# A re-planned token-and-channel mixer: one load waits for another, a copy of r goes ahead of casts of v, weight loads go ahead of batch 1's loads

## The chip, the cores and the metric

The kernel runs on one NeuronCore of one Trainium2 chip. The metric is the device time of one execution in microseconds (us). The changed kernel is compared with the kernel before by the medians of repeated executions on the same chip.

## What is computed

Four batches of a linear attention with decay (RWKV style; 8 heads, 768 steps, 48 features per head) feed an MLP mixer of token and channel parts. Cut to what matters:

```python
for t in range(S):                                   # S = 768
    kt, vt, rt = k[:, :, t], v[:, :, t], r[:, :, t]
    cur = einsum('bhd,bhe->bhde', u * kt, vt)
    y[:, :, t] = einsum('bhd,bhde->bhe', rt, state + cur)
    state = w * state + einsum('bhd,bhe->bhde', kt, vt)
x = y as (4, 768, 8 * 48 = 384)
h = (relu(x.T @ w_tok1) @ w_tok2).T                  # 768 -> 256 -> 768 over the steps
u = x + h
out = u + relu(u @ w_ch1) @ w_ch2                    # 384 -> 1536 -> 384
```

All inputs and the output are float32 in HBM.

## The kernel before

**Units.** A batch is cut into 6 chunks of 128 steps; batches and chunks are counted from 0, as in the code (the title of the change calls them one, two). A chunk needs k, v and r: tiles `kt`, `vt` (192 KB each) and, in batches 0 and 1, `win`, which holds r of two chunks (384 KB); in batches 2 and 3 `rt` (192 KB). k and r are scaled by tables of powers of w (`kr`), turned (by TensorE through `trk` and `tr_ps` in batches 0 and 1, by a DMA transpose into `rk` later), and copied out of PSUM as `rka` (k) and `rkb` (r). v is cast to `vb`. Then come the scores `at_ps`, masked to `AT` on DVE, the state `kv_ps` kept as `S`, the chunk's own step (`adg`, then `ydb` or `yd`), and `y_ps`, which is copied to `x_b`.

**Mixer.** A batch's six `x_b` go through the hidden layer (`hid`: 12 matmuls of 384 columns on `h_ps<-x_b,wtok`), back (`hx_ps` or `hT_ps`, then `uT`), 24 *up* steps (three matmuls `z_ps<-uT,wch` each and a relu to `zr`), and 18 *down* steps (four matmuls `h_ps<-wch,zr` each), then the sum `osb` and a store. The mixer of one batch is what TensorE does between the short attention steps of the next.

**Weights.** Seven loads on GpSimd's queue, which also cast to bf16: W0 and W1 (`wtok`), W2 (`wch`, columns of w_ch1 for the first 4 of 12 up steps of a half), W3 (the other 8, 768 KB), W4, W5, W6 (`wch`, a third of w_ch2 each). All but W3 are 384 KB. The hidden layer needs W0, back needs W1, up steps need W2 or W3, a down step needs one of W4 to W6.

**What sets the order.** Everything is a task of a static plan: ORDER is the order in which the tasks are written out, and each engine then executes its own instructions in that order and waits at the first one that isn't ready. ENGINES says which engine takes a task that two could do, BUFS which buffer it writes, FILL puts a few matmuls on zeros ahead of some early tasks. Three more tables add waits between DMAs, from landing to issue: HOLD makes a load wait for another load, W_DEP makes a weight load wait for a load, GATES makes a load wait for a weight load. A load is written (batch, chunk, i), with i = 0 for k, 1 for r, 2 for v. All loads, the DMA transposes and nearly all stores share SP's queue; the weight loads stand on POOL's, between its products. A wait of one load therefore holds all that stand behind it on SP.

Of the kernel before, what the change touches and what calls it, by code (L numbers as in the profile page):

```python
# [63 lines left out]
    0, 1, 2, 0, 1, 0, 2, 1, 0, 2, 1, 0, 2, 1, 0, 1, 2, 1, 0, 2, 1, 0, 2, 1,  # L64
],
    'AT1': [
    0, 1, 2, 0, 1, 0, 2, 1, 0, 2, 0, 1, 2, 1, 0, 1, 2, 0, 1, 2, 0, 1, 2, 0,
# [11 lines left out]
    0, 1, 2, 3, 4, 1, 0, 2, 3, 4, 1, 0, 2, 3, 4, 0, 1, 2, 3, 0, 4, 1, 2, 3,  # L79
# [5 lines left out]
    0, 1, 2, 3, 4, 5, 0, 1, 4, 2, 3, 0, 4, 5, 1, 2, 0, 3, 5, 1, 4, 2, 0, 3, 5, 1, 2, 0, 4, 3,  # L85
],
    'kt': [
    0, 1, 2, 3, 4, 5, 0, 1, 2, 3, 4, 5, 0, 1, 2, 3, 4, 5, 0, 2, 1, 3, 4, 5,
],
    'ku': [  # L90
    0, 1, 2, 0, 1, 0, 2, 0, 1, 2, 0, 1,
# [12 lines left out]
],  # L104
    'osb': [
    0, 1, 2, 0, 1, 2, 2, 1, 0, 1, 2, 2, 0, 1, 2, 0, 1, 0, 2, 0, 1, 2, 0, 1, 2,
# [5 lines left out]
    0, 1, 2, 3, 0, 1, 2, 3, 1, 0, 2, 3,  # L112
],
    'rka': [
    0, 1, 2, 0, 1, 2, 0, 1, 2, 0, 1, 2,
# [5 lines left out]
    0, 1, 1, 0, 1, 1, 0, 1, 0, 1, 0, 1,  # L121
],
    'rt': [
    0, 1, 2, 3, 4, 0, 1, 2, 3, 0, 4, 2,
],
    'uT': [
    0, 1, 2, 3, 1, 0, 3, 2,
# [5 lines left out]
    0, 1, 2, 3, 4, 0, 1, 3, 2, 4, 0, 1, 3, 2, 4, 3, 1, 0, 2, 3, 4, 1, 0, 3,  # L133
],
    'vt': [
    0, 1, 2, 3, 4, 5, 0, 1, 3, 2, 4, 5, 0, 1, 3, 2, 5, 4, 0, 3, 1, 2, 4, 5,
# [5 lines left out]
    0, 1, 2, 0, 2, 1, 0, 2, 1, 2, 0, 2, 0, 1, 2, 0, 1, 2,  # L142
],
    'ydb': [
    0, 1, 0, 1, 0, 1,
# [5 lines left out]
ENGINES = [  # L151
# [9 lines left out]
]  # L161
W_DEP = [(0, 2, 2), (0, 5, 0), (0, 5, 0), (0, 3, 2), (1, 2, 0), (1, 1, 2), (1, 5, 0)]
HOLD = {(0, 4, 1): (0, 2, 1),
# [12 lines left out]
GATES = {(2, 0, 2): 1, (2, 4, 1): 3, (3, 1, 0): 2, (3, 1, 1): 6, (3, 5, 2): 5}  # L176
# [1058 lines left out]
```

## Time and profile before

| what | value |
|---|---|
| times of the kernel before | 163.26, 163.88, 171.22 us (median 163.88) |
| profiled execution, device time | 163.55 us |
| its span, first to last instruction | 161.8 us |
| around the span | 1.75 us |
| busy: PE, DVE, ACT, POOL | 153.7, 114.1, 68.3, 85.7 us |
| bytes moved by DMA | 26.89 MB |

The durations below come from the profiled execution, whose time is 0.33 us under the median. TensorE (PE) is the busiest engine. Its matmuls are pipelined, so the mean duration of one (326 ns for 384 columns) is longer than the step from one to the next (about 163 ns in a row of nine such matmuls that takes 1.46 us). All lines of the kernel read L282 in the profile, since a helper records every instruction; tiles tell them apart.

### The profile page before, as it was taken

The numbers are of one execution on the slowest core, as the hardware profiler recorded it, in microseconds if no ns is written. First come the engines' busy times: TensorE is split into PE (matmuls) and PEld (weight loads), VectorE is DVE, ScalarE is ACT, GpSimd is POOL, SyncE is SP. The second block draws the span as 40 slices with busy tenths as digits, with TensorE's granted clock in tenths as the row PEclk, the third lists the DMA queues.
The fourth block names the chain that finished last, engine by engine and source line by source line (L and its number), as shares of the span: only waits on it lengthen the run. The fifth ranks groups of instructions, "written<-read, shape, count | busy, mean of one in ns | idle before, by whom it ended". The sixth has DMA issues, their size and how long they took to land.

```text
span 161.8 us, 3784 instructions
## 1 busy us (share of the span) xinstructions
PE 153.7 (95%) x1459; PEld 102.2 (63%) x1459; DVE 114.1 (70%) x243; ACT 68.3 (42%) x153; POOL 85.7 (53%) x108
## 2 busy tenths in 40 slices
PE   6998789899999899999999999999999999999992
PEld 1465567567666677666677765677666666666671
DVE  6689874568888998598799927967899245743423
ACT  3989785727732441246146341046541202242200
POOL 7149892008581179999959895999924000000000
PEclk9999999999999999999999999999999999999999
DMA  4999899998989899999999799898990143500133
GB/s 126 202 205 182 138 236 222 209 231 165 231 153 221 177 203 175 239 199 145 199 237 203 173 234 169 169 233 177 170 267 21 48 88 131 150 26 0 44 142 106
DMA packets 93061, 26.89 MB, mean 166 GB/s; under 512 B 87794, under 2 KB 92148, under 8 KB 93044
## 3 DMA queue, kind: packets, MB, share of 16 engines
q1 hardware_dynamic: 90688, 23.40, 70.6%
q0 software_dynamic: 2160, 3.15, 11.3%
q8 instruction: 11, 0.18, 0.5%
q10 hardware_dynamic: 196, 0.11, 0.2%
q14 instruction: 6, 0.05, 0.1%
HBM read 20.46 MB, written 4.72 MB: 156 GB/s over the span
## 4 chain that ended last, share of the span: by engine, by line
PE 65%; DMA 22%; DVE 3%; ACT 3%; SPq 2%; issue 1%; POOL 1%; POOLq 0%
PE h_ps L282 30%; PE z_ps L282 24%; DMA wch<-in_moe_w_ch_dram 9%; DMA kt<-in_k_dram 8%; DMA vt<-in_v_dram 5%; PE hT_ps L282 3%; PE y_ps L282 3%; PE at_ps L282 3%; SPq L282 2%; DVE AT L282 2%; PE kv_ps L282 1%; PE hx_ps L282 1%; DVE S L282 1%; ACT vb L282 1%; POOL kr L282 1%
## 5 line engine op out<-in xcount | busy, mean ns | idle before, releaser
L282 PE MATMUL h_ps<-wch,zr 128*128 128x384 bf16 (+1 forms) x300 | 54.0, 319 | 0.7 <-DMA wch<-in_moe_w_ch_dram 0.5
L282 PE MATMUL z_ps<-uT,wch 128*128 128x384 bf16 x288 | 52.0, 326 | 0.6 <-DMA wch<-in_moe_w_ch_dram 0.6
L282 ACT ACTIVATE zr<-z_ps 128x384 bf16<-128x384 f32 x59 | 27.6, 494 | 46.8 <-PE z_ps L282 39.4
L282 PEld LDWEIGHTS <-wch 128*128 128x128 bf16 x288 | 31.4, 114 | 13.8 <-DMA wch<-in_moe_w_ch_dram 1.0
L282 PEld LDWEIGHTS <-zr 128*128 128x128 bf16 x300 | 27.3, 97 | 16.0 <-issue 0.7
L282 DVE TENSOR_TENSOR AT<-at_ps,mask 128x512 bf16<-128x512 f32 x48 | 31.1, 683 | 5.4 <-PE at_ps L282 5.2
L282 DVE TENSOR_SCALAR zr<-z_ps 128x384 bf16<-128x384 f32 x37 | 19.6, 552 | 10.6 <-PE z_ps L282 9.5
L282 POOL TENSOR_TENSOR kr<-kt,wnat 128x384 bf16<-128x384 f32 x19 | 18.9, 1003 | 3.2 <-DMA kt<-in_k_dram 2.5
L282 POOL TENSOR_TENSOR yd<-vb,adg 128x384 f32<-128x384 bf16 x15 | 12.4, 834 | 8.7 <-DVE adg L282 3.9
L282 DVE TENSOR_TENSOR osb<-u_sb,h_ps 128x384 f32<-128x384 bf16 (+1 forms) x16 | 8.2, 525 | 10.7 <-PE h_ps L282 10.4
L282 PEld LDWEIGHTS <-kr 128*128 128x128 bf16 x176 | 12.0, 103 | 5.6 <-POOL kr L282 2.2
L282 ACT CAST vb<-vt 128x384 bf16<-128x384 f32 x19 | 9.6, 512 | 8.7 <-DMA vt<-in_v_dram 8.7
L282 POOL TENSOR_TENSOR rku<-ku,rt 128x384 f32<-128x384 f32 x12 | 12.0, 1012 | 1.0 <-DVE adg L282 0.9
L282 POOL TENSOR_TENSOR kr<-rt,wp 128x384 bf16<-128x384 f32 x12 | 12.2, 1036 | 0.0
L282 POOL TENSOR_TENSOR kr<-win,wpair 128x384 bf16<-128x384 f32 x4 | 4.9, 1230 | 13.5 <-DMA win<-in_r_dram 13.5
L282 POOL TENSOR_TENSOR ku<-kt,u_bc 128x384 f32<-128x384 f32 x12 | 12.0, 1009 | 0.0
L282 DVE TENSOR_TENSOR x_b<-y_ps,yd 128x384 bf16<-128x384 f32 x18 | 9.6, 549 | 2.1 <-PE y_ps L282 1.8
L282 PEld LDWEIGHTS <-wtok 128*128 128x128 bf16 x78 | 7.4, 98 | 4.3
L282 DVE TENSOR_TENSOR u_sb<-x_b,hT_ps 128x384 bf16<-128x384 bf16 x15 | 7.7, 549 | 3.4 <-PE hT_ps L282 3.4
L282 PE MATMUL h_ps<-x_b,wtok 128*128 128x384 bf16 x48 | 8.8, 326 | 0.0
L282 PE MATMUL y_ps<-vb,AT 128*128 128x48 bf16 x192 | 8.7, 183 | 0.0
L282 PEld LDWEIGHTS <-AT 128*128 128x128 bf16 x192 | 7.1, 96 | 0.3
(96 smaller groups left out, 181.8 us busy)
## 6 DMA issues: line engine op xcount, KB each, us to landing
kt<-in_k_dram SPq DMA_DIRECT2D x24, 192.0 KB, 4.1
vt<-in_v_dram SPq DMA_DIRECT2D x24, 192.0 KB, 3.7
out_dram<-osb SPq DMA_DIRECT2D x23, 192.0 KB, 2.5
win<-in_r_dram SPq DMA_DIRECT2D x6, 384.0 KB, 5.2
rt<-in_r_dram SPq DMA_DIRECT2D x12, 192.0 KB, 3.6
wch<-in_moe_w_ch_dram POOLq DMA_DIRECT2D x4, 384.0 KB, 6.6
wtok<-in_moe_w_tok_dram POOLq DMA_DIRECT2D x2, 384.0 KB, 5.6
wch<-in_moe_w_ch_dram POOLq DMA_DIRECT2D x1, 768.0 KB, 11.3
```

Of the source, the lines that this page charges most:

```text
L282: return lambda *args, **kw: tc.keep_in_program_order(f(*args, **kw))
```

## The change

Only tables change; the tasks, their number and their sizes stay. The hand-made part stands in three tables (the rest of the diff is ORDER from the 135th task on, BUFS and ENGINES, which follow from a new planning and of which two lines are shown):

```diff
-W_DEP = [(0, 2, 2), (0, 5, 0), (0, 5, 0), (0, 3, 2), (1, 2, 0), (1, 1, 2), (1, 5, 0)]
+W_DEP = [(0, 2, 2), None, (0, 4, 2), (0, 1, 0), (0, 5, 2), None, (0, 1, 0)]
 HOLD = {(0, 4, 1): (0, 2, 1),
...
         (0, 5, 0): (0, 2, 2),
-        (0, 5, 2): (0, 3, 2),
+        (0, 5, 2): (0, 2, 2),
         (1, 0, 1): (0, 4, 2),
         (1, 0, 0): (0, 5, 0)}
-GATES = {(2, 0, 2): 1, (2, 4, 1): 3, (3, 1, 0): 2, (3, 1, 1): 6, (3, 5, 2): 5}
+GATES = {(1, 1, 2): 3, (1, 2, 0): 2, (1, 4, 2): 4, (1, 5, 0): 4, (2, 1, 1): 3, (2, 2, 2): 5, (2, 3, 1): 0, (2, 3, 2): 0, (2, 5, 0): 4, (3, 0, 0): 6, (3, 0, 2): 0, (3, 1, 0): 4, (3, 3, 2): 3, (3, 5, 2): 4}
 'AT0': [
-    0, 1, 2, 0, 1, 0, 2, 1, 0, 2, 1, 0, 2, 1, 0, 1, 2, 1, 0, 2, 1, 0, 2, 1,
+    0, 1, 2, 0, 1, 0, 2, 1, 0, 2, 0, 1, 0, 2, 1, 0, 2, 1, 0, 2, 1, 0, 2, 1,
```

What this does to the engines' own orders is shown at three places.

**SP, from the last v load of batch 0 on.** The rows are SP's DMAs in order, with the semaphores that each waits for; DMASW2, DMASW3 and DMASW4 are the landings of W2, W3 and W4, a DMAHW is the landing of an earlier load, Pool, DVE and Activation that an engine is done with a buffer. Before, from (0,5,2) on: v of batch 0 chunk 5; r and k of batch 1 chunk 0; its v; r and k of chunk 2; v of chunks 1 and 2; k of chunk 1; r of chunk 4; k of chunk 3.

```order
L282 DMA vt<-in_v_dram 128x8x48 [waits DMAHW7_49]
L282 DMA win<-in_r_dram 128x8x96 [waits DMAHW0_49,DVE_49]
L282 DMA kt<-in_k_dram 128x8x48 [waits DMAHW1_49,DVE_49]
L282 DMA vt<-in_v_dram 128x8x48 [waits Activation_49]
L282 DMA win<-in_r_dram 128x8x96
L282 DMA kt<-in_k_dram 128x8x48 [waits DVE_49]
L282 DMA vt<-in_v_dram 128x8x48 [waits Activation_49] x2
L282 DMA kt<-in_k_dram 128x8x48 [waits DMAHW2_49,Pool_49]
L282 DMA win<-in_r_dram 128x8x96 [waits DMAHW3_49,DVE_49]
L282 DMA kt<-in_k_dram 128x8x48 [waits DMAHW4_49,Pool_49]
```

In the change, from the same load on: v of batch 0 chunk 5; r and k of batch 1 chunk 0; k and r of chunk 2; k of chunk 3; v of chunk 0; k and v of chunk 1; k of chunk 4; v of chunk 2; r of chunk 4.

```order
L282 DMA vt<-in_v_dram 128x8x48
L282 DMA win<-in_r_dram 128x8x96 [waits DMAHW0_49,DVE_49]
L282 DMA kt<-in_k_dram 128x8x48 [waits DMAHW1_49,DVE_49]
L282 DMA kt<-in_k_dram 128x8x48 [waits DMASW2_49,DVE_49]
L282 DMA win<-in_r_dram 128x8x96
L282 DMA kt<-in_k_dram 128x8x48 [waits DMAHW7_49,Pool_49]
L282 DMA vt<-in_v_dram 128x8x48 [waits Activation_49]
L282 DMA kt<-in_k_dram 128x8x48 [waits Pool_49]
L282 DMA vt<-in_v_dram 128x8x48 [waits DMAHW2_49,DMASW3_49,Activation_49]
L282 DMA kt<-in_k_dram 128x8x48 [waits DMAHW3_49,Pool_49]
L282 DMA vt<-in_v_dram 128x8x48 [waits DMAHW4_49,Activation_49]
L282 DMA win<-in_r_dram 128x8x96 [waits DMAHW5_49,DVE_49]
```

The v load of batch 0 chunk 5 no longer waits for a landing of its own, all of batch 1 from chunk 2's k on stands behind W2's landing, v of chunk 0 has moved back past three loads, and v of chunk 1 waits for W3. A little later k of chunk 5 waits for W4.

**POOL, from W0 on.** POOL's products and weight loads in order; `wtok_101` is W1, `wch_0_102` is W2, `wch_1_103` W3, the three `wch_104` W4 to W6; `ydb` and `yd` are chunks' own steps, `kr<-kt` and `kr<-win` scale k and r. Before:

```order
L282 DMA wtok_100<-in_moe_w_tok_dram 128x6x256
L282 TENSOR_TENSOR ydb<-vb,adg 128x384 x2
L282 TENSOR_TENSOR kr_71<-kt,wnat_84 128x8x48
L282 DMA wtok_101<-in_moe_w_tok_dram 128x1536
L282 TENSOR_TENSOR ydb<-vb,adg 128x384 x2
L282 DMA wch_0_102<-in_moe_w_ch_dram 128x3x512
L282 DMA wch_1_103<-in_moe_w_ch_dram 128x3x1024
L282 TENSOR_TENSOR kr_67<-win,wpair 128x8x48 x2
L282 DMA wch_104<-in_moe_w_ch_dram 128x1536
L282 TENSOR_TENSOR yd<-vb,adg 128x384
L282 TENSOR_TENSOR kr_72<-kt,wnat_84 128x8x48
L282 TENSOR_TENSOR kr_68<-win,wpair 128x8x48
```

In the change:

```order
L282 DMA wtok_100<-in_moe_w_tok_dram 128x6x256
L282 TENSOR_TENSOR ydb<-vb,adg 128x384 x2
L282 TENSOR_TENSOR kr_71<-kt,wnat_84 128x8x48
L282 DMA wtok_101<-in_moe_w_tok_dram 128x1536
L282 DMA wch_0_102<-in_moe_w_ch_dram 128x3x512
L282 TENSOR_TENSOR ydb<-vb,adg 128x384 x2
L282 DMA wch_1_103<-in_moe_w_ch_dram 128x3x1024
L282 TENSOR_TENSOR kr_67<-kt,wnat_84 128x8x48
L282 DMA wch_104<-in_moe_w_ch_dram 128x1536
L282 TENSOR_TENSOR kr_68<-kt,wnat_84 128x8x48
L282 DMA wch_104<-in_moe_w_ch_dram 128x1536 x2
L282 TENSOR_TENSOR kr_71<-kt,wnat_84 128x8x48
```

W2 has moved ahead of two own steps, and W3 stays behind both; W4 now waits on POOL for the scaling of chunk 2's k alone, and W5 and W6 for that of chunk 3's k.

**ACT, in batch 0's last chunks.** ACT's copies in order, from the copy of `adg` of chunk 2 on; `rkb` here is r of chunks 4 and 5, the casts to `vb` are v of chunks 3, 2, 4 before and 2, 3, 4 in the change. Before:

```order
L282 COPY adg<-ad_ps 128x8
L282 CAST vb<-vt 128x384 x2
L282 COPY rkb<-tr_ps 128x1024
L282 CAST vb<-vt 128x384
L282 CAST x_b_98<-y_ps 128x384
```

In the change:

```order
L282 COPY adg<-ad_ps 128x8
L282 COPY rkb<-tr_ps 128x1024
L282 CAST vb<-vt 128x384 x2
L282 CAST S_0_96<-kv_ps 48x4x48 x2
L282 CAST vb<-vt 128x384
L282 CAST x_b_98<-y_ps 128x384 x3
```

The copy of r has moved past two casts of v, and DVE in turn takes the copy of k (`rka`) and the state of later chunks of batch 0, while ACT takes the cast of chunk 5's v.

More of the change, by code (lines that the diff above doesn't have):

```diff
@@ L63 @@
     'AT0': [
-    0, 1, 2, 0, 1, 0, 2, 1, 0, 2, 1, 0, 2, 1, 0, 1, 2, 1, 0, 2, 1, 0, 2, 1,
+    0, 1, 2, 0, 1, 0, 2, 1, 0, 2, 0, 1, 0, 2, 1, 0, 2, 1, 0, 2, 1, 0, 2, 1,
 ],
     'AT1': [
-    0, 1, 2, 0, 1, 0, 2, 1, 0, 2, 0, 1, 2, 1, 0, 1, 2, 0, 1, 2, 0, 1, 2, 0,
+    0, 1, 2, 0, 1, 0, 2, 1, 0, 2, 1, 0, 1, 2, 0, 2, 1, 0, 2, 0, 1, 2, 0, 1,
 ],
@@ L78 @@
     'adg': [
-    0, 1, 2, 3, 4, 1, 0, 2, 3, 4, 1, 0, 2, 3, 4, 0, 1, 2, 3, 0, 4, 1, 2, 3,
+    0, 1, 2, 3, 4, 1, 2, 0, 3, 4, 1, 2, 0, 3, 4, 1, 2, 3, 1, 4, 3, 0, 2, 1,
 ],
@@ L84 @@
     'kp': [
-    0, 1, 2, 3, 4, 5, 0, 1, 4, 2, 3, 0, 4, 5, 1, 2, 0, 3, 5, 1, 4, 2, 0, 3, 5, 1, 2, 0, 4, 3,
+    0, 1, 2, 3, 4, 5, 0, 1, 4, 2, 3, 0, 5, 1, 4, 2, 3, 5, 4, 0, 3, 1, 5, 2, 4, 3, 1, 0, 5, 2,
 ],
     'kt': [
-    0, 1, 2, 3, 4, 5, 0, 1, 2, 3, 4, 5, 0, 1, 2, 3, 4, 5, 0, 2, 1, 3, 4, 5,
+    0, 1, 2, 3, 4, 5, 0, 1, 2, 3, 4, 5, 0, 1, 2, 3, 4, 0, 5, 1, 2, 3, 0, 4,
 ],
     'ku': [
-    0, 1, 2, 0, 1, 0, 2, 0, 1, 2, 0, 1,
+    0, 1, 2, 0, 1, 0, 2, 0, 1, 2, 0, 2,
 ],
@@ L96 @@
     'm': [
[7 rows of a table removed]
[7 rows of a table added]
 ],
     'osb': [
-    0, 1, 2, 0, 1, 2, 2, 1, 0, 1, 2, 2, 0, 1, 2, 0, 1, 0, 2, 0, 1, 2, 0, 1, 2,
+    0, 1, 2, 1, 0, 2, 2, 1, 0, 0, 2, 2, 2, 0, 1, 0, 0, 0, 2, 1, 0, 2, 1, 0, 2,
 ],
@@ L111 @@
     'rk': [
-    0, 1, 2, 3, 0, 1, 2, 3, 1, 0, 2, 3,
+    0, 1, 2, 3, 0, 1, 3, 2, 0, 1, 2, 3,
 ],
     'rka': [
-    0, 1, 2, 0, 1, 2, 0, 1, 2, 0, 1, 2,
+    0, 1, 2, 0, 1, 0, 2, 1, 0, 2, 1, 0,
 ],
@@ L120 @@
     'rku': [
-    0, 1, 1, 0, 1, 1, 0, 1, 0, 1, 0, 1,
+    0, 1, 0, 1, 0, 1, 1, 0, 0, 1, 0, 1,
 ],
     'rt': [
-    0, 1, 2, 3, 4, 0, 1, 2, 3, 0, 4, 2,
+    0, 1, 2, 3, 4, 1, 2, 3, 0, 1, 4, 2,
 ],
     'uT': [
-    0, 1, 2, 3, 1, 0, 3, 2,
+    0, 1, 2, 3, 0, 1, 2, 3,
 ],
@@ L132 @@
     'vb': [
-    0, 1, 2, 3, 4, 0, 1, 3, 2, 4, 0, 1, 3, 2, 4, 3, 1, 0, 2, 3, 4, 1, 0, 3,
+    0, 1, 2, 3, 4, 0, 1, 2, 3, 4, 0, 1, 2, 4, 0, 3, 1, 2, 4, 0, 1, 2, 3, 4,
 ],
     'vt': [
-    0, 1, 2, 3, 4, 5, 0, 1, 3, 2, 4, 5, 0, 1, 3, 2, 5, 4, 0, 3, 1, 2, 4, 5,
+    0, 1, 2, 3, 4, 5, 0, 1, 2, 3, 4, 5, 0, 1, 2, 3, 5, 4, 0, 1, 2, 3, 5, 4,
 ],
@@ L141 @@
     'yd': [
-    0, 1, 2, 0, 2, 1, 0, 2, 1, 2, 0, 2, 0, 1, 2, 0, 1, 2,
+    0, 1, 2, 0, 1, 2, 0, 1, 2, 0, 1, 2, 1, 0, 2, 1, 0, 1,
 ],
     'ydb': [
-    0, 1, 0, 1, 0, 1,
+    0, 1, 0, 0, 1, 0,
 ],
```

98 rows, old and new, of tables (BUFS, ENGINES, ORDER) are left out of this document.

## The prediction

> **What bounds the kernel now.** First the page: which engine is full, and over which part of the span.
>
> ```profile
> span 161.8 us, 3784 instructions
> ...
> PE 153.7 (95%) x1459; PEld 102.2 (63%) x1459; DVE 114.1 (70%) x243; ACT 68.3 (42%) x153; POOL 85.7 (53%) x108
> ...
> DMA  4999899998989899999999799898990143500133
> ...
> PE 65%; DMA 22%; DVE 3%; ACT 3%; SPq 2%; issue 1%; POOL 1%; POOLq 0%
> ```
>
> PE is busy 95% of the span and owns 65% of the chain that ended last, but DMA owns 22% of it, and DMA is near full from the second slice to the thirtieth. So the question is where PE stands still for a load. The view of busy time by stage answers it (columns: stage, its length, busy us of PE, PEld, DVE, ACT, POOL; then clock, DMA share and GB/s).
>
> ```profile
> 12.00:24.00 12.00, 9.89 (x165) 6.70 (x165) 10.20 (x24) 10.19 (x28) 10.79 (x13) 1.00 1.03 182
> 24.00:32.00 8.00, 7.29 (x86) 5.12 (x84) 4.22 (x9) 5.03 (x13) 1.48 (x2) 1.00 1.19 219
> 32.00:40.00 8.00, 8.00 (x62) 5.45 (x61) 5.73 (x12) 4.03 (x11) 2.88 (x3) 1.00 0.99 194
> 40.00:56.00 16.00, 15.05 (x173) 10.57 (x171) 14.27 (x30) 7.31 (x18) 7.11 (x8) 1.00 1.02 199
> 56.00:118.00 62.00, 62.00 (x628) 42.53 (x627) 49.17 (x94) 24.67 (x59) 55.70 (x59) 1.00 1.02 194
> 118.00:125.00 7.00, 6.94 (x90) 4.64 (x89) 6.74 (x16) 1.74 (x4) 2.45 (x3) 1.00 0.58 152
> ```
>
> From 56 us on PE never rests until its last matmul: 62.00 of 62.00, then 6.94 of 7.00. All that a new order can win lies before: 0.71 us between 24 and 32, 0.95 us between 40 and 56, together **1.66 us**, and 2.11 us between 12 and 24, where the first chunks' chains run. That is the ceiling; there is no floor, since PE executes in order and any load that comes late adds its lateness in full. DMA is also busy all along (182 to 219 GB/s), so a weight that goes ahead makes some k, r or v late by the same bytes.
>
> PE's timeline names the waits (last column: idle time before, and who ended it), and the chain in order of time tells what stood behind them.
>
> ```profile
> 20.57 0.40 PE L282 MATMUL at_ps<-rkb,rka 64*128 64x128 bf16 x8 [0.58 <-ACT rkb L282]
> ...
> 31.56 0.68 PE L282 MATMUL z_ps<-uT,wch 128*128 128x384 bf16 x3 [0.62 <-DMA wch<-in_moe_w_ch_dram]
> ...
> 43.38 0.40 PE L282 MATMUL trk<-ident,kr 128*128 128x128 bf16 x4 [0.32 <-POOL kr L282]
> ...
> 53.52 0.81 PE L282 MATMUL h_ps<-wch,zr 128*128 128x384 bf16 x4 [0.54 <-DMA wch<-in_moe_w_ch_dram]
> ```
>
> ```profile
> 23.05 0.77 POOL ydb L282
> 23.82 7.69 DMA wch<-in_moe_w_ch_dram
> ...
> 36.76 5.44 DMA kt<-in_k_dram
> 42.19 0.03 issue
> 42.22 0.02 POOLq L282
> 42.24 0.09 issue
> 42.33 1.01 POOL kr L282
> ...
> 44.05 1.46 PE z_ps L282 x9
> ...
> 46.94 6.54 DMA wch<-in_moe_w_ch_dram
> ```
>
> Three waits of 0.62 (W2), 0.32 (k of batch 1 chunk 1) and 0.54 us (W6) make 1.48 of the 1.66 us.
>
> **The change part by part.** PE's work is the same before and after: no matmul is added or dropped.
>
> *W2 earlier.* POOL sent it at 23.82, behind two own steps:
>
> ```profile
> 21.43 0.61 POOL L282 DMA_DIRECT2D wtok<-in_moe_w_tok_dram  x1
> 22.06 0.84 POOL L282 TENSOR_TENSOR ydb<-vb,adg 128x384 bf16<-128x384 bf16 x1
> 23.05 0.83 POOL L282 TENSOR_TENSOR ydb<-vb,adg 128x384 bf16<-128x384 bf16 x1 [0.15 <-ACT adg L282]
> 23.82 1.65 POOL L282 DMA_DIRECT2D wch<-in_moe_w_ch_dram  x2
> ...
> 39.32 0.66 POOL L282 DMA_DIRECT2D wch<-in_moe_w_ch_dram  x1
> ...
> 44.94 0.61 POOL L282 DMA_DIRECT2D wch<-in_moe_w_ch_dram  x1
> ...
> 46.94 0.59 POOL L282 DMA_DIRECT2D wch<-in_moe_w_ch_dram  x1 [0.36 <-PE ad_ps L282]
> ```
>
> Now it follows W1 at once, at 21.43 + 0.61 = 22.0, that is 1.8 us sooner, and lands near 31.5 - 1.8 = 29.7. The wait of 0.62 us goes. Next late is batch 0's own chain (last `x_b`, hidden layer, back, `uT`), which ended PE's previous work 0.62 us before; the first up step can gain between 0 and 0.62 us: I take **-0.4**, near the upper end, since one more back step than before now stands ahead of it.
>
> *r ahead of v, and the last v load of batch 0.* On ACT and SP:
>
> ```profile
> 17.46 0.17 ACT L282 COPY adg<-ad_ps 128x8 f32<-128x8 f32 x1
> 18.69 0.93 ACT L282 CAST vb<-vt 128x384 bf16<-128x384 f32 x2 [1.07 <-DMA vt<-in_v_dram]
> 19.52 1.00 ACT L282 COPY rkb<-tr_ps 128x1024 bf16<-128x1024 bf16 x1
> ```
>
> ```profile
> 16.29 0.37 SPq L282 DMA_DIRECT2D kt<-in_k_dram  x1
> 18.68 0.37 SPq L282 DMA_DIRECT2D vt<-in_v_dram  x1
> ```
>
> ACT stood 1.07 us for a v, then copied r, and PE waited 0.58 us for that copy. Now the copy runs at 17.63 to 18.63, inside that wait, and the score starts up to 1.9 us sooner. But DVE, 10.20 of 12 us busy in this stage, gets a copy of k and a state that ACT had, so what is late next is DVE's masks. I take **0**, with bounds of +-0.6 (the wait itself, won, or lost to DVE). The v load of chunk 5 stood on SP from 16.66 to 18.68 and leaves up to 2.0 us sooner, but no row shows PE waiting for its cast: 0, between the same bounds.
>
> *W4 to W6 earlier.* Before they left at 39.32, 44.94 and 46.94. Now k of chunk 2 leaves at W2's landing (29.7), behind the 768 KB of W3, which take 0.79 MB / 0.2 MB per us = 4 us; it lands near 34.5, POOL scales it in 1.0 us (the row at 42.33), and W4 leaves at about 36, W5 and W6 after chunk 3's k at about 39. W6 took 6.54 us from issue to landing in the chain above, so it is there by 46, or by 48 behind the other two. PE reaches the first down step after 24 up steps of 1.46 / 3 = 0.49 us and some 1.2 us of attention, near 31.2 + 11.7 + 1.2 = 44, and the first one that needs W6 some 5 us later. So the wait of 0.54 goes, and that of 0.32 for chunk 1's k too, as that turn now stands behind all up steps: **-0.86**, or nothing if W6 is as late as before.
>
> *Loads of batch 1 later.* This is the price. Between W2's issue and the last weight, the DMA view of one stage shows how two queues share:
>
> ```profile
> q0 software_dynamic: 695, 1.06, 97.4%
> q1 hardware_dynamic: 561, 0.20, 17.2%
> ```
>
> From 28 to 34 us the weights (q0) moved 1.06 MB and the loads (q1) 0.20 MB, though loads were waiting: a `win` issued in that time's run-up took
>
> ```profile
> win<-in_r_dram SPq DMA_DIRECT2D x1, 384.0 KB, 13.6
> ```
>
> 13.6 us to land. [...]
>
> Now v of chunk 0, k of chunk 1 and v of chunk 1 come behind k, r and k of chunks 2 and 3 (0.79 MB, 4 us after W3, so until about 38), just when W4 to W6 take over. Three weights of 0.39 MB at (1.06 / 6 = 0.18 MB per us) take 6.7 us, in which loads get 0.22 MB, one k or v. So v of chunk 0 lands near 39, k of chunk 1 at 43 to 45, v of chunk 1 at 45 to 46. PE wants the first at about 41, the second (after scaling) at 45.5, the third at 46.5. That is just in time for two of three: I take **+0.6** for one short stall, with bounds 0 and 3.5 (v of chunk 0 waiting for all three weights too: 38 + 6.7 = 45 against 41).
>
> *Later tables.* The same tasks, the mixer's downs spread otherwise, POOL with 3 more own steps of batch 1 in a stage where it is busy 7.11 of 16 us: 0, between 0 and the third rival's price.
>
> *Sum:* -0.4 + 0 - 0.86 + 0.6 = -0.66 on 163.55 us: **162.9 us**. The profiled execution is 0.33 us under the median shown. About 2% (3.3 us) is what a measurement of this kernel can tell from no change.
>
> **The rivals.** *The weights starve batch 1* (slower). Place: v of chunk 0, whose cast stands on DVE ahead of relus of up steps, and k and v of chunk 1. For it speaks the row of 13.6 us; against it that v of chunk 0 is the fourth load behind W2's landing and W4 cannot leave before chunk 2's k is scaled. It decides once v of chunk 0 lands after about 41 us: PE stands up to 3.5 us there and 1 us more at chunk 1, the 1.3 us are won all the same: 163.55 - 1.3 + 3.5 = 165.8, at worst 167 when it meets twice.
>
> *All is won and nothing paid.* No stall of batch 1's loads, and the early stage gains its 0.6: 163.55 - 1.66 - 0.6 = 161.3. For more, PE would have to be idle elsewhere, which the stage rows exclude.
>
> *The gain is given back later.* Between 56 and 118 us POOL is busy 55.70 of 62 and DMA at 1.02, and batch 3's last masks end just as PE needs them (the 0.06 us of 118 to 125). If loads or POOL's products of batches 2 and 3 are no earlier than before, PE waits there for what it won: 163.55, no change; POOL behind by 2 us gives 165.5.
>
> *The dependency alone does nothing.* The named first edit frees one load; behind it r and k of batch 1 keep their own holds. That is no time of its own; it only says that the effect, if any, is the weights'.
>
> **How the numbers follow.** Forecast (162.9; 162.2 to 163.4): 0.50. Starvation (165.8; 163.6 to 168): 0.27, of which 0.12 is over 166.8. Given back (163.5; up to 165.5): 0.16, of which 0.02 over. All won (161.3): 0.07, of which 0.03 under 160.3, from an early stage that gains more than I can see. Faster by over 2%: 0.03; slower by over 2%: 0.15, with 0.01 for a later stall that I don't see; within: 0.82. The range reaches from 161.3 to 167.0.
>
> **What would show it.** Right: no wait for `wch` at the first up step, W4 to W6 issued before 40 us, PE busy over 15.5 of 16 us between 40 and 56, and at most one wait under 1 us for a k or v of batch 1. Wrong: DVE or PE waiting for `vt` or `kt` between 40 and 50 (starvation), or PE idle after 56 us, which it was not before (given back). A wait for W3 near 35 us would mean that W3, still behind two own steps, has become what W2 was.

## The result, and the profile after

| | kernel before | kernel after |
|---|---|---|
| median of 19 executions each | 164.17 us | 163.29 us |
| profiled execution, device time | 163.55 us | 162.31 us |
| its span | 161.8 us | 160.6 us |

The ratio of the executions is **0.9937, 95% interval 0.991 to 0.9963**: about 1.0 us faster (164 x 0.0063). The interval excludes no difference, but the change is well inside the 2% that the prediction's chances count as no change. The forecast was 162.9 us, -0.66 us. Over all comparisons 13 of 106 executions of the kernel before took more than 166.5 us, against none of 19 of the kernel after and one of 84 of the seven variants of it that leave W4 to W6 in their places on POOL; a ratio leaves such executions out where a kernel has shorter ones too.

First the page of the kernel after: span, busy time, and who owns the chain that ended last.

```profile
span 160.6 us, 3775 instructions
...
PE 153.1 (95%) x1458; PEld 102.6 (64%) x1459; DVE 112.6 (70%) x241; ACT 67.4 (42%) x151; POOL 88.1 (55%) x112
...
PE 82%; DMA 5%; DVE 5%; POOL 2%; issue 1%; SPq 1%; ACT 1%; DVEq 0%; ACTq 0%; POOLq 0%
```

DMA owned 22% of the chain before and owns 5% now; PE's share went from 65 to 82%. The view of busy time by stage of the kernel after (stage, length, busy us of PE, PEld, DVE, ACT, POOL, clock, DMA share, GB/s) says where:

```profile
12.00:24.00 12.00, 9.02 (x156) 6.23 (x157) 10.22 (x23) 8.64 (x23) 9.68 (x11) 1.00 1.02 184
24.00:32.00 8.00, 7.98 (x96) 5.68 (x94) 6.41 (x15) 5.37 (x13) 2.40 (x3) 1.00 1.12 193
...
40.00:56.00 16.00, 16.00 (x186) 11.43 (x185) 11.42 (x24) 8.18 (x20) 9.99 (x11) 1.00 1.01 202
56.00:118.00 62.00, 61.84 (x623) 42.35 (x621) 47.44 (x94) 26.76 (x64) 54.94 (x59) 1.00 1.08 201
118.00:125.00 7.00, 7.00 (x92) 4.76 (x91) 6.54 (x14) 1.31 (x3) 2.49 (x3) 1.00 0.43 94
```

Against the rows of before PE won 0.69 us between 24 and 32 and all 0.95 us between 40 and 56. It lost 0.87 us between 12 and 24, and 0.10 us after 56. Of the 0.87 us, 0.21 are no loss: a matmul on zeros near 14.6 us has no record in the trace of after, though its weight load has one. With that the stages add up to 0.88 us, while the device times of the two profiled executions differ by 1.24 us; a lone matmul of 384 columns counts as busy for 0.33 us, twice the 0.163 us after which the next one follows in a row, so busy time hides short waits.

PE's timeline shows the new early wait (last column), and what stands ahead of the first up step:

```profile
20.05 0.26 PE L282 MATMUL ad_ps<-u_blk,pr 128*128 128x8 bf16 x4 [1.08 <-DVE pr L282]
...
30.27 1.14 PE L282 MATMUL hx_ps<-wtok,h1r 128*128 128x384 bf16 x6
31.25 0.39 PE L282 MATMUL trk<-ident,kr 128*128 128x128 bf16 x4
31.47 0.81 PE L282 MATMUL z_ps<-uT,wch 128*128 128x384 bf16 x4
```

The first up step has no wait for `wch` any more, but it starts at 31.47, against 31.56 before: only 0.09 us sooner. One more back step (two matmuls, 0.33 us) is done by then, so batch 0's chain is 0.42 us further. What was lost before, at chunk 4's product (`pr`) above all, went into the slack that W2's wait had been.

POOL's timeline of the kernel after has the weights: W2, W3, then W4 behind the scaling of chunk 2's k, W5 and W6 behind that of chunk 3's.

```profile
22.68 0.75 POOL L282 DMA_DIRECT2D wch<-in_moe_w_ch_dram  x1
...
26.72 0.81 POOL L282 DMA_DIRECT2D wch<-in_moe_w_ch_dram  x1
...
36.56 0.60 POOL L282 DMA_DIRECT2D wch<-in_moe_w_ch_dram  x1
38.21 1.16 POOL L282 TENSOR_TENSOR kr<-kt,wnat 128x384 bf16<-128x384 f32 x1 [1.05 <-DMA kt<-in_k_dram]
39.33 1.14 POOL L282 DMA_DIRECT2D wch<-in_moe_w_ch_dram  x2
```

W6 left at 39.93 instead of 46.94 and landed at 48.08 instead of 53.48; the first down step that reads it waits for nothing:

```profile
48.87 0.82 PE L282 MATMUL h_ps<-wch,zr 128*128 128x384 bf16 x4
```

### The profile page after: what moved, and what is told of

Read it like the earlier page. It is cut to its first block, busy times and chain, and to the rows that moved or that the text cites. A ratio compares the mean times of both kernels' runs of the same rounds, so it can differ in the third digit from the quotient of the medians.

```text
span 160.6 us, 3775 instructions
## 1 busy us (share of the span) xinstructions
PE 153.1 (95%) x1458; PEld 102.6 (64%) x1459; DVE 112.6 (70%) x241; ACT 67.4 (42%) x151; POOL 88.1 (55%) x112
## 4 chain that ended last, share of the span: by engine, by line
PE 82%; DMA 5%; DVE 5%; POOL 2%; issue 1%; SPq 1%; ACT 1%; DVEq 0%; ACTq 0%; POOLq 0%
PE h_ps L282 34%; PE z_ps L282 29%; DMA kt<-in_k_dram 5%; PE y_ps L282 5%; PE at_ps L282 4%; PE hT_ps L282 3%; PE hx_ps L282 3%; PE kv_ps L282 2%; POOL kr L282 2%; DVE AT L282 1%; SPq L282 1%; PE trk L282 1%; DVE S L282 1%; DVE pr L282 1%; ACT S L282 1%
## 5 line engine op out<-in xcount | busy, mean ns | idle before, releaser
L282 PE MATMUL h_ps<-wch,zr 128*128 128x384 bf16 (+1 forms) x300 | 54.3, 320 | 0.0
L282 PE MATMUL z_ps<-uT,wch 128*128 128x384 bf16 x288 | 51.8, 326 | 0.0
L282 ACT ACTIVATE zr<-z_ps 128x384 bf16<-128x384 f32 x62 | 28.3, 492 | 43.1 <-PE z_ps L282 43.0
L282 PEld LDWEIGHTS <-wch 128*128 128x128 bf16 x288 | 31.7, 114 | 13.0
L282 PEld LDWEIGHTS <-zr 128*128 128x128 bf16 x300 | 27.2, 97 | 15.4 <-issue 0.2
L282 DVE TENSOR_TENSOR AT<-at_ps,mask 128x512 bf16<-128x512 f32 x48 | 31.1, 684 | 5.6 <-PE at_ps L282 5.3
L282 POOL TENSOR_TENSOR kr<-kt,wnat 128x384 bf16<-128x384 f32 x21 | 21.0, 1007 | 13.8 <-DMA kt<-in_k_dram 13.1
L282 DVE TENSOR_SCALAR zr<-z_ps 128x384 bf16<-128x384 f32 x34 | 18.5, 554 | 13.0 <-PE z_ps L282 13.0
L282 POOL TENSOR_TENSOR yd<-vb,adg 128x384 f32<-128x384 bf16 x18 | 14.9, 830 | 9.4 <-ACT vb L282 2.9
L282 PEld LDWEIGHTS <-kr 128*128 128x128 bf16 x176 | 12.1, 103 | 4.9 <-POOL kr L282 1.6
L282 DVE TENSOR_TENSOR osb<-u_sb,h_ps 128x384 f32<-128x384 bf16 (+1 forms) x16 | 8.3, 525 | 6.5 <-PE h_ps L282 4.6
L282 POOL TENSOR_TENSOR rku<-ku,rt 128x384 f32<-128x384 f32 x12 | 12.0, 1004 | 0.5 <-DVE adg L282 0.4
L282 ACT CAST vb<-vt 128x384 bf16<-128x384 f32 x22 | 10.9, 513 | 2.9 <-DMA vt<-in_v_dram 2.6
L282 POOL TENSOR_TENSOR ku<-kt,u_bc 128x384 f32<-128x384 f32 x12 | 12.0, 1004 | 0.0
L282 POOL TENSOR_TENSOR kr<-rt,wp 128x384 bf16<-128x384 f32 x12 | 11.9, 1002 | 0.0
L282 DVE TENSOR_TENSOR x_b<-y_ps,yd 128x384 bf16<-128x384 f32 x18 | 9.6, 550 | 1.5 <-PE y_ps L282 1.1
L282 PEld LDWEIGHTS <-wtok 128*128 128x128 bf16 x78 | 7.4, 98 | 4.4
L282 DVE TENSOR_TENSOR u_sb<-x_b,hT_ps 128x384 bf16<-128x384 bf16 x15 | 7.8, 550 | 2.9 <-PE hT_ps L282 2.7
L282 ACT ACTIVATE h1r<-h_ps 128x384 bf16<-128x384 f32 x4 | 2.0, 491 | 17.2 <-PE h_ps L282 17.2
L282 PE MATMUL h_ps<-x_b,wtok 128*128 128x384 bf16 x48 | 8.8, 326 | 0.0
L282 PE MATMUL y_ps<-vb,AT 128*128 128x48 bf16 x192 | 8.8, 183 | 0.0
L282 PEld LDWEIGHTS <-AT 128*128 128x128 bf16 x192 | 7.2, 96 | 0.2
```

Of the source, the lines that this page charges most:

```text
L282: return lambda *args, **kw: tc.keep_in_program_order(f(*args, **kw))
```

## The experiments

Rows of the variants say L284 where the two kernels say L282; it is the same recording helper. "Against the kernel after" compares two ratios to the kernel before, 0.01 of which is 1.6 us; such a difference is uncertain by 0.7 to 0.9 us.

**W5 and W6 late again.** The kernel after with two weight loads moved on POOL:

```diff
 wch_104 (W4)
 kr of b1 c3
-wch_104 x2 (W5, W6)
 kr of b1 c1
 yd of b1 c0
+wch_104 (W5)
 pr of b1 c1
+wch_104 (W6)
```

> The kernel after, with W5 sent only behind the own step of batch 1 chunk 0 and W6 behind the product of batch 1 chunk 1 on POOL, that is at about 43 and 47 us instead of 39.33 and 39.93; W2, W3, W4 stay where they are. Theory (the gain of 40 to 56 us is W5's and W6's earlier issue): PE waits for W6 again at the first down step that needs it, which now stands earlier than it did before (about 48.9 us), while W6 lands near 53; the time rises by 1 to 4.8 us and the row of 40 to 56 us shows PE idle by as much. The rival (the moment of the weights doesn't matter, the new order of attention and mixer does it): no change, within 0.3 us.

Measured: median 167.23 us, ratio 1.0204 (1.0154 to 1.0254), 4.4 us over the kernel after. Its timeline of PE and of POOL:

```profile
49.06 1.46 PE L284 MATMUL h_ps<-wch,zr 128*128 128x384 bf16 x8 [1.39 <-DMA wch<-in_moe_w_ch_dram]
52.68 0.81 PE L284 MATMUL h_ps<-wch,zr 128*128 128x384 bf16 x4 [1.60 <-DMA wch<-in_moe_w_ch_dram]
```

```profile
43.99 0.61 POOL L284 DMA_DIRECT2D wch<-in_moe_w_ch_dram  x1
47.79 0.59 POOL L284 DMA_DIRECT2D wch<-in_moe_w_ch_dram  x1
```

Two waits for weights, 1.39 and 1.60 us; the time rose by more than their sum, to the upper end of the theory. The profiled execution is 3.8 us longer than that of the kernel after: 3.0 us for the two waits, and by an estimate from the matmuls done about 0.5 us already lost at 44 us, with a granted clock of 0.90 from 12 to 24 us and 0.94 from 24 to 32. The rival (order alone) is out: with the order of attention and mixer of the kernel after, 4 to 8 us of delay of these two loads cost more than the whole change brings.

**W4 to W6 still earlier.** The kernel after with all three behind W3:

```diff
 wch_1_103 (W3)
+wch_104 x3 (W4, W5, W6)
 kr of b1 c2
-wch_104 (W4)
 kr of b1 c3
-wch_104 x2 (W5, W6)
```

> The kernel after, with W4, W5 and W6 sent right behind W3, at about 27.5 us instead of 36.56, 39.33 and 39.93; all else stays. It puts 1.2 MB of weights, some 6.5 us at 0.18 MB per us, ahead of the loads of batch 1 chunks 2 and 3 and v of chunk 0. The starvation rival: those loads get a sixth of the bytes until about 41 us, k of chunk 2 lands near 40 instead of 35.52 and v of chunk 0 near 44; PE waits for them between 40 and 50 us and the time rises by 3 to 5 us. The prediction's +0.6 us, which wasn't paid with the weights at 36 to 40 us, would be paid here in full. Against it (loads of batch 1 have several us to spare): within 0.5 us of the kernel after.

Measured: median 168.57 us, ratio 1.0265 (1.0207 to 1.0323), 5.4 us over the kernel after. Rows of PE and of DVE, and the two queues between 28 and 41 us (packets, MB, share of 16 engines):

```profile
44.03 0.25 PE L284 MATMUL ad_ps<-u_blk,pr 128*128 128x8 bf16 x4 [2.88 <-DVE zr L284]
```

```profile
42.95 0.56 DVE L284 TENSOR_TENSOR kr<-win,wpair 128x384 bf16<-128x384 f32 x1 [4.13 <-DMA win<-in_r_dram]
```

```profile
q0 software_dynamic: 1184, 2.31, 95.7%
q1 hardware_dynamic: 1642, 0.43, 15.9%
```

The weights moved 2.31 MB while the loads got 0.43. DVE stood 4.13 us for r of chunks 2 and 3, with relus of up steps behind it, and PE stood for such a relu. So starvation is real, and in this plan dearer than the prediction's rival had it (165.8 us, at worst 167), but its first victim is that r, not v of chunk 0. The kernel after doesn't pay it: W4 leaves 9 us later there (36.56 against 27.91). That kernel's queues in two windows show how narrow it is:

```profile
q1 hardware_dynamic: 1730, 0.33, 105.5%
...
q0 software_dynamic: 144, 0.39, 99.1%
q1 hardware_dynamic: 97, 0.02, 7.8%
...
kt<-in_k_dram SPq DMA_DIRECT2D x1, 192.0 KB, 10.6
```

The first row is 36 to 38 us: no weight moves at all, though W4 was issued at 36.56, and v of chunk 0 and k and v of chunk 1 get through. The next two are 44 to 46 us: the weights have everything. The last row is k of chunk 4, issued at 37.73, which took 10.6 us to land; nothing on PE waits for it.

**W5 and W6 early in the kernel before.**

```diff
 wch_104 (W4)
+wch_104 x2 (W5, W6)
 yd of b1 c0
 ...
-wch_104 (W5)
 ...
-wch_104 (W6)
-W_DEP = [..., (1, 2, 0), (1, 1, 2), (1, 5, 0)]
+W_DEP = [..., (1, 2, 0), None, None]
```

> The kernel before, with W5 and W6 written out right behind W4 and without their waits for a k load of batch 0 or 1; all else stays. POOL sends them at about 40 us instead of 44.94 and 46.94. Theory (a late W6 is worth what PE waited for it): W6 lands by about 48 to 50 us instead of 53.48, the wait of 0.54 us at the first down step of that third goes, and so does whatever stood at W5; the time falls by 0.5 to 0.8 us. The rival (weights starve batch 1's loads): three weights in a row hold loads of batch 1 that before lay between them, and k of chunk 1, which PE already waits for by 0.32 us, or v of chunk 2 comes 1 us or more later; the time rises by 0.5 us or more.

Measured: median 165.64 us; six executions between 163.1 and 164.4 (ratio 0.9992, 0.9953 to 1.0031) and six between 166.9 and 170.0. The profiled execution is one of the longer six; its PE row:

```profile
52.40 0.61 PE L284 MATMUL trk<-ident,kr 128*128 128x128 bf16 x4 [3.94 <-POOL kr L284]
```

The scaling it waits for had waited 7.18 us on POOL for a k of batch 1. That is the rival's mechanism. The gain of 0.5 to 0.8 us isn't seen in the shorter six either, though their interval (0.77 us less to 0.51 more) doesn't rule it out. So neither theory is borne out as stated: where the weights go early in the old order of loads, no gain is seen and half of the executions lose some 5 us. Why only half is open.

**W2 early in the kernel before.**

```diff
 wtok_101 (W1)
+wch_0_102 (W2)
 ydb x2
-wch_0_102 (W2)
 wch_1_103 (W3)
-W_DEP = [(0, 2, 2), (0, 5, 0), (0, 5, 0), ...]
+W_DEP = [(0, 2, 2), None, (0, 4, 2), ...]
```

> The kernel before, with one thing of the change: W2 is written right behind W1 on POOL, ahead of two own steps (with the change's own waits for W1 and W2), at about 22 us instead of 23.82; W3 and all else stay. Theory: W2 lands near 30 instead of 31.51, the wait of 0.62 us at the first up step goes, and the first up step starts up to 0.62 us sooner; since DMA is full there (1.19 between 24 and 32 us) part of it may come back at k of batch 1 chunk 1, so the time falls by 0 to 0.6 us. Rival (batch 0's own chain ends no sooner, as the kernel after shows with a first up step at 31.47 against 31.56): PE waits for that chain instead and the time stays within 0.15 us.

Measured: median 170.32 us, ratio **1.0393** (1.0346 to 1.0441), all six executions between 168.9 and 171.0. Both theories fail. A row of PE, one of stage, and the issue of k of batch 1 chunk 0 (KB, us to landing):

```profile
35.03 0.61 PE L284 MATMUL trk<-ident,kr 128*128 128x128 bf16 x4 [5.62 <-DVE kr L284]
```

```profile
24.00:32.00 8.00, 5.33 (x64) 3.63 (x59) 2.62 (x6) 3.35 (x9) 0.89 (x2) 1.00 1.16 205
```

```profile
kt<-in_k_dram SPq DMA_DIRECT2D x1, 192.0 KB, 14.4
```

The k took 14.4 us to land, in the kernel before 8.3 us, in the kernel after 6.3 us:

```profile
kt<-in_k_dram SPq DMA_DIRECT2D x1, 192.0 KB, 8.3
```

```profile
kt<-in_k_dram SPq DMA_DIRECT2D x1, 192.0 KB, 6.3
```

So W2 ahead of two own steps, without the other parts of the change, costs 6.5 us (164 x 0.0393). (W1's wait is gone too, but W1 left at 21.15 instead of 21.43.) In that trace the k was issued from 19.96 to 22.29 us, and W1, W2 and W3 left at 21.15, 21.75 and 24.07, on top of it; PE wants that k at 29.4 us in that order of work, ahead of the last back step. In the kernel after the k is issued in full by 20.61, W1 leaves only at 22.08 and W3 at 26.72, and the turn of that k stands behind the last back step, at 31.25.

The traces of all fourteen kernels bear this out. In the five in which that k was issued in full before W1 left, it landed 6.3 to 6.6 us after its issue began. In the nine in which W1 left while it was being issued, it took 6.1 to 14.4 us, in eight of them 8.3 or more.

**The same, with the first edit of the change** (the last v load of batch 0 waits for v of chunk 2):

```diff
-        (0, 5, 2): (0, 3, 2),
+        (0, 5, 2): (0, 2, 2),
```

> The kernel before with two things of the change: W2 right behind W1, and the last v load of batch 0 waiting for v of chunk 2 instead of v of chunk 3. With W2 alone, k of batch 1 chunk 0 was issued from 19.96 to 22.29 us, across W1 and W2, landed at 34.39, and PE waited 5.62 us for it. Theory (the freed load takes its place on SP out of the way of that k, which then leaves before W1, as in the kernel after, where it was issued from 19.92 to 20.61 and landed at 26.21): k lands before 29 us, the wait goes, and the time is that of the kernel before or up to 0.6 us under it. Rival (the hold has nothing to do with it, W2 itself starves the k): k lands near 34 us again and the time stays some 6 us above the kernel before.

Measured: median 165.38 us; six executions between 162.8 and 165.0 (ratio 0.9994, 0.9947 to 1.0041), one at 165.8, five between 169.7 and 171.8. The profiled execution is one of the long five, and has the same wait:

```profile
35.26 0.61 PE L284 MATMUL trk<-ident,kr 128*128 128x128 bf16 x4 [5.51 <-DVE kr L284]
```

With W2 alone no execution of six escaped, with the earlier v load about half of twelve do, on another chip. That speaks weakly for the freed load as a help; in the profiled execution W1 and W2 left while the k was being issued, as with W2 alone. In the six short ones no gain is seen against the kernel before, though their interval (0.87 us less to 0.67 more) leaves room for W2's 0.62 us. What decides between the short and the long ones is not shown.

**The first edit taken out of the kernel after** (the same lines the other way round).

> The kernel after, with the first edit of the change undone: the last v load of batch 0 waits for the landing of v of chunk 3 again, instead of v of chunk 2. It stands on SP ahead of r and k of batch 1 chunk 0, which wait for earlier landings of their own. Theory: the load leaves up to 2 us later, its cast (at 25.30 us on ACT) has time to spare, and nothing moves: within 0.3 us of the kernel after. Rival (SP is held and batch 1's first loads come later): r of batch 1 chunk 0 lands after 26 us, its turn on PE at 28.3 us waits, +0.5 us or more.

Measured: median 163.47 us, ratio 0.9973 (0.9943 to 1.0002), which can't be told from the kernel after. But in its trace one load comes much later: the issue of the same k

```profile
kt<-in_k_dram SPq DMA_DIRECT2D x1, 192.0 KB, 10.7
```

took 3.85 us on SP instead of 0.69, and it landed at 30.90 us instead of 26.21; it was scaled by 31.48, 0.4 us before its turn on PE at 31.88. So the load arrives just in time here, and with over 4 us to spare in the kernel after. That the edit alone does this is not shown: with the edit in place the same k landed at 31.01 us in the variant below with ACT's copy put back, and at 29.12 in the one with scalings on POOL, and in both W1 left while it was being issued. Two things besides stand in this profile that the kernel after's own does not have. PE's clock, by windows of 2 us:

```profile
18.00:20.00 2.00, 0.99 (x22) 0.56 (x18) 1.48 (x4) 1.83 (x3) 0.45 (x2) 1.00 0.95 136
20.00:22.00 2.00, 1.86 (x29) 1.46 (x30) 1.70 (x5) 1.14 (x3) 2.00 (x3) 0.67 1.32 178
22.00:24.00 2.00, 2.00 (x31) 1.65 (x29) 1.16 (x3) 0.00 (x0) 1.44 (x3) 0.50 1.41 278
```

And DVE beside POOL near 40 us, with the wait on PE that followed:

```profile
38.60 1.21 DVE L284 TENSOR_TENSOR kr<-win,wpair 128x384 bf16<-128x384 f32 x1
39.73 0.54 DVE L284 TENSOR_SCALAR zr<-z_ps 128x384 bf16<-128x384 f32 x1
40.20 1.74 DVE L284 TENSOR_TENSOR kr<-win,wpair 128x384 bf16<-128x384 f32 x1
```

```profile
38.40 0.99 POOL L284 TENSOR_TENSOR kr<-kt,wnat 128x384 bf16<-128x384 f32 x1 [1.06 <-DMA kt<-in_k_dram]
39.35 1.14 POOL L284 DMA_DIRECT2D wch<-in_moe_w_ch_dram  x2
40.49 1.02 POOL L284 TENSOR_TENSOR kr<-kt,wnat 128x384 bf16<-128x384 f32 x1
```

```profile
42.46 0.65 PE L284 MATMUL z_ps<-uT,wch 128*128 128x384 bf16 x3 [0.85 <-DVE zr L284]
```

Both are taken up by the experiments below.

**Batch 1's waits for weights taken out of the kernel after.**

```diff
-GATES = {(1, 1, 2): 3, (1, 2, 0): 2, (1, 4, 2): 4, (1, 5, 0): 4, (2, 1, 1): 3, ...}
+GATES = {(2, 1, 1): 3, ...}
```

> The kernel after without the four waits of batch 1's loads for weights (k of chunk 2 for W2, v of chunk 1 for W3, v of chunk 4 and k of chunk 5 for W4); the order of SP and all else stay. Loads of batch 1 may then leave while W0 to W3 are under way. Theory (the waits keep the weights ahead): k of chunk 2 leaves some 8 us earlier, W1 and W2 land later by what batch 1's loads take of the bytes, PE waits at the hidden layer's second half (W1, 28.2 us) or at the first up step (W2), and the time rises by 0.3 to 1.5 us. Rival (by the sixth of the bytes that loads get beside a weight, as between 28 and 34 us before): weights lose almost nothing, the time stays within 0.3 us.

Measured: median 163.78 us, ratio 1.0007 (0.9975 to 1.004), 1.1 us over the kernel after. k of chunk 2 left at 21.96 instead of 30.12, W2 landed at 31.15 instead of 30.06 and W3 at 36.93 instead of 34.48. The size is the theory's, the place isn't: no matmul waits for a weight. PE stands for the cast of v of chunk 0,

```profile
43.02 0.33 PE L284 MATMUL kv_ps<-vb,kr 128*128 128x96 bf16 x4 [0.38 <-DVE vb L284]
```

and 7 of the 12 executions have a lower mean clock (0.987 to 0.989, more of this below), the profiled one too: by an estimate from the matmuls done it fell 1.1 us behind the kernel after between 20 and 28 us, where the clock granted in windows of 2 us was 0.93, 0.50, 0.71 and 1.00. So what these waits are worth by themselves is open.

**ACT's copy of r back behind the casts of v.** In the kernel after:

```diff
 L282 COPY adg<-ad_ps 128x8
-L282 COPY rkb<-tr_ps 128x1024
 L282 CAST vb<-vt 128x384 x2
+L282 COPY rkb<-tr_ps 128x1024
```

> The kernel after, with the copy of r (`rkb` of batch 0's chunks 4 and 5) on ACT back behind the casts of v of chunks 2 and 3, as before; DVE's product of chunk 4, which reads it, stands behind it. The copy then starts near 19.0 us instead of 18.04. Theory (the prediction's 0 for this edit): what PE waits for in 12 to 24 us is DVE, the scores of chunk 4 come 0.5 to 1 us later, the end of batch 0 moves by less, and the time rises by 0 to 0.5 us. Rival (the copy is what lets batch 0 end at 31.4 us in spite of DVE's new work): it rises by 0.9 us or more.

Measured: median 164.12 us, ratio 1.0001 (0.9969 to 1.0033), 1.0 us over the kernel after: the rival, though the uncertainty reaches into the theory's range. PE's wait at chunk 4's product grew from 1.08 us:

```profile
20.80 0.27 PE L284 MATMUL ad_ps<-u_blk,pr 128*128 128x8 bf16 x4 [1.82 <-DVE pr L284]
```

Its clock fell to half from 21 to 27 us in the profiled execution (0.59 between 20 and 22 us, 0.50 up to 26, 0.70 up to 28), and 8 of the 12 have a lower mean clock (0.979 to 0.99), so how wait and clock share the 1.0 us is open.

**PE's sum of chunk 4 behind its scores.** In the kernel after, PE's order:

```diff
-sum over pr, chunk 4     (ad_ps<-u_blk,pr)
 state, chunk 2           (kv_ps<-S,ident)
 scores, chunk 4          (at_ps<-rkb,rka)
+sum over pr, chunk 4
```

> The kernel after, with one PE task of batch 0 chunk 4 (the sum over the product `pr`, four matmuls of 8 columns on `ad_ps`) written behind that chunk's scores instead of ahead of them. PE waited 1.08 us there for DVE's product (at 20.05 us). Theory A (the early stage is bound by PE standing in order behind that wait): the scores start 1 us sooner, DVE's mask too, and batch 0 ends earlier; the time falls by up to 0.9 us, the 0.87 us that 12 to 24 us lost. Theory B (DVE, 10.22 of 12 us busy there, sets the pace): the mask comes no sooner, the time stays within 0.2 us.

Measured: median 163.44 us, ratio 0.9967 (0.9937 to 0.9996), not to be told from the kernel after. The stages say that both theories are half right:

```profile
12.00:24.00 12.00, 9.86 (x164) 6.55 (x164) 10.34 (x24) 9.13 (x24) 9.67 (x11) 1.00 0.97 169
24.00:32.00 8.00, 7.41 (x83) 5.26 (x83) 5.73 (x14) 4.77 (x12) 2.41 (x3) 1.00 1.17 216
...
40.00:56.00 16.00, 15.12 (x174) 10.76 (x172) 11.71 (x22) 7.00 (x19) 8.52 (x10) 1.00 1.05 207
```

The 0.84 us won between 12 and 24 come back as 0.57 us between 24 and 32, where PE waits for W1, and as 0.88 us between 40 and 56, the same wait for a relu behind DVE's scalings as in the variant above (1.23 and 1.74 us there too).

**Those scalings on POOL.** In the kernel after, ENGINES gives two tasks to POOL:

```diff
 wch_104 (W4)
+kr<-win, first half
 kr of b1 c3
 wch_104 x2 (W5, W6)
+kr<-win, second half
 kr of b1 c1
```

> The kernel after, with the two scalings of r of batch 1 chunks 2 and 3 (`kr<-win`) taken from DVE and given to POOL, the first behind W4, the second behind W6. In the kernel after they took 0.55 and 0.90 us on DVE beside POOL's own scalings of k, in two variants of it 1.2 and 1.74 us, and PE then waited 1.0 us near 41 us for a relu. Theory (DVE stands still while POOL multiplies, so the median of the kernel after holds part of that 1.0 us, though its profile doesn't): DVE has no two-input product there, the row of 40 to 56 us shows PE busy 16 of 16 in every execution, and the time falls by 0.3 to 1.0 us against the kernel after. Rival (the scalings merely move, W5 and W6 leave 1 us later and k of chunk 1 is scaled 1 us later): W6 lands near 49 us, just too late, and the time rises by 0.2 to 1 us.

Measured: median 163.06 us, ratio 0.9946 (0.9917 to 0.9974): no difference from the kernel after. The row of 40 to 56 us is 16.00 of 16, so the rival's late W6 (it landed at 48.40) didn't come; neither did the theory's gain. The wait for the relu is thus a loss of some variants; that the kernel after's median holds any of it is not shown.

**Both, and both with W1 earlier.** The two edits above together:

> The kernel after with both edits: the sum over the product of batch 0 chunk 4 behind its scores on PE, and the two scalings of r of batch 1 chunks 2 and 3 on POOL. The first won 0.84 us between 12 and 24 us and gave it back as 0.57 us at W1 (28.3 us) and 1.04 us near 41 us. Theory: with the second edit the 1.04 us goes and the time is 0.3 to 1.2 us under the kernel after. Rival (each stage's gain is taken by the next load, W1 or W2 or W6): no more than 0.3 us.

Measured: median 162.51 us (161.93 to 163.61), ratio 0.9931 (0.9903 to 0.996). And with W1 behind the own step of chunk 2:

> The same two edits, and W1 written two products earlier on POOL (behind the own step of batch 0 chunk 2), near 20 us instead of 22. Theory (W1's landing at 28 to 29 us is what the early gain runs into): W1 lands near 27 us, the wait of 0.56 us for it goes, and the time is 0.3 to 0.6 us under that of the two edits alone. Rival (W1 meets k of batch 1 chunk 0, issued at 20 us, as W2 did in the kernel before): that k lands after 31 us instead of 26.21, PE waits for it, and the time rises by 1 us or more.

Measured: median 162.73 us, ratio 0.9919 (0.9882 to 0.9956). Neither can be told from the kernel after or from each other. With W1 earlier the wait for it goes, but k of batch 1 chunk 0 lands at 30.65, so each of its two expectations was half met. A version better than the kernel after by more than the uncertainty was not found. What the first of them has is steadiness: none of its 12 executions has a mean clock under 0.998.

## Why the prediction was right, point by point

The sum (-0.66, measured about -1.0) and the likeliest case held. Its steps did not all hold: without the +0.6, which wasn't paid, it would be -1.26, against -1.24 in the two profiled executions. That the total fits with that term wrong is in part luck.

*What bounds the kernel: right.* The ceiling of 1.66 us after 24 us was in the right places: 0.69 and 0.95 us of it were won. The signs named came: no wait for `wch`, W4 to W6 issued before 40 us, PE busy 16.00 of 16, no wait of PE for a k or v of batch 1 between 40 and 56 us.

*W4 to W6 earlier, -0.86: right.* -0.95 in that stage. Issue at 36.56 to 39.93 (forecast 36 and 39), W6 landed at 48.08 (forecast 46, or 48 behind the others). Moving W5 and W6 back cost 4.4 us.

*W2 earlier, -0.4, bounds 0 and 0.62: the amount right, the bounds wrong.* W2 left at 22.68 and landed at 30.06 (forecast 22.0 and 29.7), its wait went, and batch 0's chain, named as next late, kept all but 0.42 us. That is what this term and the next won together, and no run puts W2 alone back in the kernel after, so W2's own share is argued from the traces. But the bounds took the edit as one that could at worst win nothing. Without the rest of the change it costs 6.5 us, since it delays k of batch 1 chunk 0. The prediction looked for starved loads among those behind W2's landing, and not at the one being issued just ahead of W2. The change escapes this by its other parts, as argued from the traces: W3 2.7 us later, that k's turn 1.8 us later on PE, and the k issued in full before W1 leaves. Which of these carries most wasn't separated.

*r ahead of v, 0 with bounds +-0.6: the sum right, the term mis-sized.* PE lost some 0.7 us to 24 us as DVE became the limit, as said ("what is late next is DVE's masks"), so the stage won nothing. The scores of chunk 4, forecast up to 1.9 us sooner, started at 20.59 us, against 20.57 before, since on PE chunk 4's sum now stands ahead of them and waits 1.08 us for DVE's product. But putting the copy back costs 1.0 us (0.36 to 1.7), so it is probably worth more than the bound, and the new plan spends that on this sum.

*Loads of batch 1 later, +0.6: not paid, and mis-sized.* The step that failed is "just when W4 to W6 take over". W4's bytes only began to move after 38 us, and the three loads had left by 37.6. k of chunk 1 landed at 40.89 (forecast 43 to 45). The loads that paid are k of chunk 4 and v of chunk 2, which nothing needs so soon. The term took the shares of 28 to 34 us (0.20 MB for the loads, 1.06 MB for the weights) as those of the later stage too, which was the author's estimate; between 36.6 and 48.1 us the loads got 1.24 MB beside 1.18. Starvation itself is real: it cost 5.4 us when W4 to W6 left at 27.9 to 29.0 us and the loads got 0.43 MB beside 2.31.

*Later tables, 0: right within 0.10 us* of PE's busy time after 56 us. "Given back later" didn't come as a whole, but some was given back on the way: by an estimate from the matmuls done, the kernel after is 1.7 us ahead at 56 us, 0.8 at 118 and 1.2 at the end. *"The dependency alone does nothing"* holds in the time of the kernel after (no measurable difference without it). What it does to the plan is open: k of batch 1 chunk 0 landed 4.7 us later without it in one trace, but later still in one that has it.

## What to carry to other kernels

A load that is moved earlier may be paid for by whichever transfer is being issued just then, as k of batch 1 chunk 0 paid here (14.4 us to land instead of 8.3): look at what is needed next on PE among those under way, not only at those queued behind it, since here the same edit cost 6.5 us in one order and went with a gain in another. When a wait vanishes, ask which chain ended just before it; here 0.62 us of wait gave 0.42. And a wait of a microsecond on PE may cost twice, once as time and once as clock: with the 1.08 us at chunk 4's product, 8 of 19 executions of the kernel after have a lower mean clock and took 0.6 us more than the others, while with that small sum behind the scores it was 1 of 36, with medians not to be told from that of the kernel after.

## What was not expected of the hardware

**The clock after a short wait.** In the rows above PE was busy 0.99 of 2 us, and one window later its granted clock was 0.67, then 0.50, for about 3 us; between 24 and 26 us it was 0.98. The kernel after and four variants that leave chunk 4's sum ahead of its scores (the first edit taken out, batch 1's waits taken out, ACT's copy back, the scalings on POOL; the wait there was 1.08 us in the kernel after and in the first of them, 1.82 with ACT's copy back) have a mean clock under 0.995 in 33 of 67 executions, 8 of 19 in the kernel after; the three that move that sum, in 1 of 36. In each of the five kernels the executions with the lower clock took 0.5 to 0.8 us more in the mean than the others, in the kernel after 163.6 us against 163.0. The profiled execution of the kernel after is one without the lower clock (0.97 of 2 us busy, then clock 1.00), so the profile alone didn't show it. So a wait of 1.08 us went with the lower clock in one profiled execution and not in the other, and what decides it no run here shows. By the records PE was busy 0.99 of 2 us and 1.86 of the next 2 where the clock fell, 0.97 and 1.74 where it didn't.

**DVE's scaling beside POOL's product.** DVE's scaling of r takes 0.55 us (the median of nine in the kernel after). With the first edit taken out it took 1.21 and 1.74 us beside POOL's products, and in both cases it ended 0.42 to 0.43 us after POOL's product did (39.39 and 39.81, 41.51 and 41.94). In the kernel after the same pair took 0.55 and 0.90, a matter of 0.6 us in when the first starts:

```profile
37.96 0.55 DVE L282 TENSOR_TENSOR kr<-win,wpair 128x384 bf16<-128x384 f32 x1
...
38.90 0.90 DVE L282 TENSOR_TENSOR kr<-win,wpair 128x384 bf16<-128x384 f32 x1
```

The second of these ended 0.43 us after POOL's product too (39.37 and 39.80). The trace counts the added time as busy time of DVE. That DVE stands still while POOL multiplies is the author's reading of these ends. Which of the two yields isn't clear from them: in the second case above DVE had started 0.29 us before POOL's product, and still ended after it.

**How two queues share.** Between 36.6 and 48.1 us weights moved 1.18 MB in 432 packets and loads 1.24 MB in 5760; between 28 and 34 us it was 0.92 MB in 548 and 0.20 MB in 978. Over a stage the bytes were shared about evenly in the first case and at nearly five to one in the second, and within a stage they alternate, as the windows at 36 and 44 us show. The packets that the profile counts don't go one for one in these stages, although 695 and 561 of the two queues are near it in the row of the kernel before that the prediction shows. Those of the loads hold some 200 bytes here, those of the weights 1.7 to 2.7 KB. What sets the shares no run here shows.
